# Row transform of an attention and Fourier-mixing kernel: fp32 products in place of a high and a low fp16 part

## The chip, the core and the metric

The kernel runs on one core of a Trainium2 chip. The core has TensorE (PE in the profile; PEld are its weight loads), VectorE (DVE), ScalarE (ACT), GpSimd (POOL) and SyncE (SP), which issues transfers. Each engine follows its own list of instructions in order. The metric is the device time of one launch in microseconds (us), a median over runs. SBUF is the memory beside the engines, PSUM the banks that TensorE writes products to.

## The reference

Two stages, for 4 batches, 8 heads, 768 rows and 64 values a head (8 x 64 = 512 columns):

```python
# attention in chunks of 32 rows, 16 rows of context before, 8 after, and 8 memory rows
scores = scale * np.matmul(q_c, k_full.transpose(0, 1, 3, 2))
a = np.exp(scores - np.max(scores, axis=-1, keepdims=True))
a = a / (np.sum(a, axis=-1, keepdims=True) + 1e-09)
out[:, :, c_start:c_end] = np.matmul(a, v_full)
# the heads side by side: x is (4, 768, 512)
mixed = np.real(np.fft.fft(np.fft.fft(x, axis=1), axis=2))
u = x + mixed
un = (u - mean(u)) / np.sqrt(var(u) + 1e-06)          # over the 512 columns
y = u + np.maximum(un @ w_ch1, 0.0) @ w_ch2           # 512 -> 2048 -> 512
```

The Fourier transform over the 768 rows is what the change touches. It is a sum over rows with tables of cosines and sines, so it can be done as matrix products.

## The kernel before, in words

The real part of the two-dimensional transform is symmetric, and the kernel folds the data first. For a batch, x (xs[b]) lies as 6 tiles of 128 rows by 512 columns. Columns c and c+256 are added and subtracted (zy): the sums carry the even output columns (par = 0), the differences the odd ones (par = 1). Rows r and r+384 are added and subtracted (pq): three row tiles each for even and odd row frequencies (sp = 0, 1). Columns are folded once more onto their mirror image (ff): a sum or a difference (ab = 0 for the cosine table, ab = 1 for the sine table), 128 columns each. What is left for a pair (par, ab) is 2 x 3 products (sp, and three row tiles st), each with a table of 128 rows by 193 columns (cosS, sinS). For par = 0 there is also one single column, 128, that folds onto itself and is done with six products of one column. Call six products (sp, st) a group.

Tables and data of these products are fp16. So that nothing is lost, ff (fp32) is split: ScalarE casts it to fp16 (hi, in e_hi and g_hi), VectorE subtracts (lo, in e_lo and g_lo), and TensorE takes each product twice, once with hi and once with lo, into the same PSUM bank (ps). In the profile these are lines 589 (batches 1 to 3), and 729, 735 and 748 (batch 0). ScalarE and VectorE split the result the same way into up (lines 601 and 606), and column products with tables cosD and sinD follow (pm, lines 759 and 780).

Batch 0 is done in another way (first_fourier, the functions whose names begin with g_), since its attention arrives half by half: g = 0 are row tiles 0 to 2, g = 1 tiles 3 to 5. There rows r and r+384 are not folded; each half is multiplied as it arrives, and for odd row frequencies of the second half a negated table (odd) is used. So a pair (par, ab) has 2 x 6 products, each with hi and with lo. The single columns (mid) are split on GpSimd. Their bank is first written by one product of zeros (line 729).

The other work on TensorE: the attention's turning of q and k (trq, trk, line 409), scores (sc, lines 465 and 488), values (xa and xo, line 517, in fp32), the first layer (ph, line 897), the last layer (pc, lines 915 and 964). In line 517 two products of 64 columns are written to the two halves of the partitions:

```python
nc.tensor.matmul(xa[64 * half:64 * half + 64, st, hh, 0:65],
                 e1[:, hh, t6, :], v1[:, hh, 6 * g + t6, 0:65],
                 start=True, stop=True)
```

For most pairs of row tiles (FAST) the last layer's 128x256 products (line 964) are saved by sums S that VectorE makes of the hidden values (line 952), and VectorE adds each bank to the rows (line 969).

The order of instructions is worked out when the program is built. A class Plan holds every step as a task: engine, a cost in us, the tasks it comes after, and the buffers it takes and gives back (take, give; their numbers are the slots of Plan, such as fold=2, un=6). Plan.order places tasks on the engines by rank and readiness, and Plan.shortest tries 24 variations of the ranks and keeps the one with the earliest end by those costs. The products of the last two layers are fillers that TensorE takes when nothing ranked higher is ready. Early on, before enough data is there, TensorE is given products of zeros (idle, line 1024). Buffers that matter here: fold (2 of 6 KB a partition; zy, pq, ff, later mix), hi and lo, un (normalised rows), unT (the same turned, two row tiles each), hT (hidden values).

Of the kernel before, what the change touches and what calls it, by code (L numbers as in the profile page):

```python
# [11 lines left out]
FP32 = mybir.dt.float32  # L12
BF16 = mybir.dt.bfloat16
# [193 lines left out]
def kernel(  # L207
# [70 lines left out]
    MIXED = 1  # L278
    cp_q = "p h j d -> p h (j d)"
# [5 lines left out]
                     xsb=3, fold=2, hl=1, up=4, dn=1, acc=2, mlp=2, un=6, unT=5, hT=1, S=1, room=2))  # L285
# [5 lines left out]
    mkf = fpool.tile([P, 2, D], FP32, tag="un", bufs=6, name="mkf")  # L291
    mkb = fpool.tile([P, 2 * D], BF16, tag="un", bufs=6, name="mkb")
# [11 lines left out]
    ident = fpool.tile([P, P], FP32, tag="un", bufs=6, name="ident")  # L304
# [231 lines left out]
    zy_of, pq_of, ff_of, hl_of, ps_of, up_of, pm_of, un_of, tp_of, dn_of, xr_of = ({} for _ in range(11))  # L536
    mu_of, unT_of, rs_of, rstd_of, g_of = ({} for _ in range(5))
    mid = cpool.tile([P, 2, NST, 1], FP16)
    mid32 = cpool.tile([P, NST, 1], FP32)
    warm = cpool.tile([P, 1], FP32)  # L540
# [18 lines left out]
    def e_ff(b, par, ab):  # L559
        pq = pq_of[b, par]  # L560
        if ab == 0:
            ff_of[b, par] = fpool.tile([P, 2, NST, P], FP32, tag="fold", bufs=2, name="ff")
        ff = ff_of[b, par]
        op = ALU.add if ab == par else ALU.subtract
        nc.vector.tensor_copy(ff[:, ab, :, 0], pq[:, :, P * ab])
        nc.vector.tensor_tensor(ff[:, ab, :, 1:P], pq[:, :, 1:P],  # L566
                                rev_ap(pq, HD - 1, P - 1, [[HD, NST]]), op)

    def e_hi(b, par, ab):
        if ab == 0:  # L570
            hl_of[b, par] = (fpool.tile([P, 2, NST, P], FP16, tag="hi", bufs=1, name="hi"),
                             fpool.tile([P, 2, NST, P], FP16, tag="lo", bufs=1, name="lo"))
        fl = "p b c -> p (b c)"
        nc.scalar.copy(hl_of[b, par][0][:, ab].rearrange(fl), ff_of[b, par][:, ab].rearrange(fl))  # L574

    def e_lo(b, par, ab):
        hi, lo = hl_of[b, par]
        fl = "p b c -> p (b c)"
        nc.vector.tensor_tensor(lo[:, ab].rearrange(fl), ff_of[b, par][:, ab].rearrange(fl),
                                hi[:, ab].rearrange(fl), ALU.subtract)  # L580

    def e_rows(b, par, ab):
        ps_of[b, par, ab] = ps = bank("acc", [P, 2, NK], FP32, "ps")

        def dft(out_, tab, c0, c1):
            for sp in range(2):
                for st in range(3):
                    for i, part in enumerate(hl_of[b, par]):
                        nc.tensor.matmul(out_[:, sp, :], part[:, ab, sp * 3 + st, c0:c1],  # L589
                                         tab[:, sp, st, :], start=(st == 0 and i == 0),  # L590
                                         stop=(st == 2 and i == 1))
# [107 lines left out]
    def g_hl(par, which):  # L699
        if (par, 0) not in g_of:  # L700
            if par == 0:
                g_of[0, 0] = fpool.tile([P, 2, NST, P], FP16, tag="hi", bufs=1, name="hi0")
                g_of[0, 1] = fpool.tile([P, 2, NST, P], FP16, tag="lo", bufs=1, name="lo0")
            else:
                both = fpool.tile([P, 2, 2, NST, P], FP16, tag="hT", bufs=1, name="hl1")
                g_of[1, 0], g_of[1, 1] = both[:, 0], both[:, 1]
        return g_of[par, which]

    def g_hi(par, ab, g):
        sl = slice(3 * g, 3 * g + 3)  # L710
        nc.scalar.copy(g_hl(par, 0)[:, ab, sl], ff_of[0, par][:, ab, sl])

    def g_lo(par, ab, g):
        sl = slice(3 * g, 3 * g + 3)
        nc.vector.tensor_tensor(g_hl(par, 1)[:, ab, sl], ff_of[0, par][:, ab, sl],
                                g_hl(par, 0)[:, ab, sl], ALU.subtract)

    def g_mid(g):
        sl = slice(3 * g, 3 * g + 3)
        xb = xs[0][:, sl]  # L720
        nc.gpsimd.tensor_tensor(mid32[:, sl], xb[:, :, P:P + 1], xb[:, :, HD + P:HD + P + 1],
                                ALU.add)
        nc.gpsimd.tensor_copy(mid[:, 0, sl], mid32[:, sl])
        nc.gpsimd.tensor_tensor(mid[:, 1, sl], mid32[:, sl], mid[:, 0, sl], ALU.subtract)

    def g_row(g):
        if g == 0:
            ps_of[0, 0, 1] = bank("acc", [P, 2, NK], FP32, "ps")
            nc.tensor.matmul(ps_of[0, 0, 1].rearrange("p s k -> p (s k)"), dz,
                             strided(dz, 0, [[0, NK], [1, 2]]), start=True, stop=False)  # L730
        for sp in range(2):
            one = odd[:, 0] if g == 1 and sp == 1 else cosS[:, sp]
            for st in range(3):
                for i in range(2):
                    nc.tensor.matmul(ps_of[0, 0, 1][0:1, sp, :], mid[:, i, 3 * g + st, :],
                                     one[:, st, :], start=False, stop=False)

    def g_rows(par, ab, g):
        if g == 0 and (par, ab) != (0, 1):
            ps_of[0, par, ab] = bank("acc" if par == 0 else "mlp", [P, 2, NK], FP32, "ps")  # L740
        ps = ps_of[0, par, ab]
        todo = []
        for sp in range(2):
            tab = odd[:, ab] if g == 1 and sp == 1 else (cosS, sinS)[ab][:, sp]
            todo += [(ps[:, sp, :], g_hl(par, i)[:, ab, 3 * g + st, :], tab[:, st, :])
                     for st in range(3) for i in range(2)]
        for m, (out_, data, tab) in enumerate(todo):
            nc.tensor.matmul(out_, data, tab, start=(g == 0 and m == 0 and (par, ab) != (0, 1)),  # L748
                             stop=(g == 1 and m == len(todo) - 1))
# [88 lines left out]
    def e_un(b, kt):  # L838
        un_of[b, kt] = un = fpool.tile([P, DM], FP16, tag="un", bufs=6, name="un")
# [23 lines left out]
    def unT(b, kt):  # L863
        i = kt if b == 0 else SLOT.index(kt)
        if (b, i // 2) not in unT_of:
            unT_of[b, i // 2] = fpool.tile([P, NDT, 2 * P], FP16, tag="unT", bufs=5, name="unT")
        return unT_of[b, i // 2][:, :, ts(i % 2, P)]
# [326 lines left out]
    def e_negatives():  # L1194
        for i, tab in enumerate((cosS, sinS)):
# [17 lines left out]
    t_neg = add("DVE", 0.6, e_negatives, [t_sines], rank=100)  # L1213
# [18 lines left out]
    def first_fourier():  # L1232
        t_rest, t_mid, t_row, pre = {}, {}, {}, {}
        for g in range(2):
# [18 lines left out]
            if g == 0:  # L1253
                for par in range(2):
                    for ab in range(2):
# [5 lines left out]
            t_row[g] = add("PE", 1.2, lambda g=g: g_row(g), [t_mid[g], t_neg, t_row.get(0), t_dz],  # L1261
                           take=("acc",) if g == 0 else ())
            for par in range(2):
                for ab in range(2):
# [8 lines left out]
                    if (par, ab, g) == (0, 0, 1):  # L1273
                        t_mark.append(ff)
                    hi = add("ACT", 0.5, lambda par=par, ab=ab, g=g: g_hi(par, ab, g),
                             [ff] + (pre[par, ab, 1][2:] if g == 1 else [pre[par, ab, 2]]),
                             take=(("hl",), ("hT",))[par] if (ab, g) == (0, 0) else ())
                    lo = add("DVE", 0.48, lambda par=par, ab=ab, g=g: g_lo(par, ab, g), [hi],
                             give=("fold",) if end else ())
                    if (par, ab, g) == (0, 0, 0):  # L1280
                        plan.filling = (t_sc[0, 0], add("PE", 0.0, lambda: let_go(fill_of[0]), [lo],
                                                        give=("mlp",)))
                    tag = ("acc", "mlp")[par]
                    mid_ = (par, ab) == (0, 1)
                    rw = add("PE", 1.0, lambda par=par, ab=ab, g=g: g_rows(par, ab, g),
                             [lo, t_neg] + ([t_row[g]] if mid_ else []),
                             take=(tag,) if g == 0 and not mid_ else (),
                             give=(("hl",), ("hT",))[par] if end else ())
# [9 lines left out]
    def fourier(b):  # L1298
# [7 lines left out]
        ff = hi = None  # L1306
        for par in range(2):
# [8 lines left out]
            for ab in range(2):  # L1316
                ff = add("DVE", 1.1, lambda par=par, ab=ab: e_ff(b, par, ab), [pq, prev],
                         take=("fold",) if ab == 0 else (), give=("fold",) if ab == 1 else ())
                prev = ff
                hi = add("ACT", 0.85, lambda par=par, ab=ab: e_hi(b, par, ab), [ff, hi],  # L1320
                         take=("hl",) if ab == 0 else ())
                lo = add("DVE", 0.96, lambda par=par, ab=ab: e_lo(b, par, ab), [hi],
                         give=("fold",) if ab == 1 else ())
                rw = add("PE", 2.2 if par == 0 and ab == 1 else 1.02,
                         lambda par=par, ab=ab: e_rows(b, par, ab), [lo, t_sines],
                         take=("acc",), give=("hl",) if ab == 1 else ())
# [265 lines left out]
```

## Time and profile before

| what | us |
|---|---|
| median of 3 runs (277.37 to 277.85) | 277.37 |
| the profiled execution, its own time | 277.39 |
| span in the profile, first to last instruction | 275.7 |
| TensorE busy | 258.7 |
| VectorE busy | 204.9 |
| ScalarE busy | 160.6 |
| GpSimd busy | 78.5 |

The granted TensorE clock is full speed throughout. The page divides the span into 40 slices of about 6.9 us and gives each engine's busy share in tenths. The chain of work is followed back from the last instruction: at each step to what released it, or to the instruction before it on its engine. In its list in order of time each line has the start, the length, the engine, the tile written and the line of the kernel, and how many instructions were merged. In lists by line, a name such as ps<-cosS,hi says what is written and read; 128*128 are active rows and columns of the array, 128x193 is the shape that streams through. A matmul's duration includes its run through the array; the next one starts before it ends.

### The profile page before, as it was taken

What the parts mean: (1) busy time and instruction counts of PE and PEld (TensorE: products, weight loads), DVE (VectorE), ACT (ScalarE), POOL (GpSimd) and SP (SyncE); (2) the same over time, 40 slices, a digit from 0 to 9 for tenths busy, and PEclk for the clock granted to TensorE, in tenths of its full rate; (3) what the DMA queues carried; (4) which work ended last, traced back from release to release, by engine and by line L of the source; (5) the groups of instructions that cost most, each with busy time, mean ns of one, the idle gap of its engine ahead of it and who ended that gap; (6) DMA issues with size and microseconds to landing.
All of it is one profiled execution on the core that took longest, in us unless ns stands there. A gap on an engine that the chain in (4) does not pass through costs nothing.

```text
span 275.7 us, 8160 instructions
## 1 busy us (share of the span) xinstructions
PE 258.7 (94%) x3365; PEld 209.8 (76%) x3365; DVE 204.9 (74%) x460; ACT 160.6 (58%) x300; POOL 78.5 (28%) x146
## 2 busy tenths in 40 slices
PE   0489999999999999999999989999999998999995
PEld 0367797888756788658669868888889887888884
DVE  7978999840337999998995997839997996354444
ACT  6888647888555688277646627555373483615150
POOL 8852652350111054045046246001100371000000
PEclk9999999999999999999999999999999999999999
DMA  6999999999997979958989964644960424313152
GB/s 104 203 176 176 193 211 205 198 195 200 174 190 176 204 170 175 212 79 160 241 144 199 183 118 117 123 117 146 132 182 1 95 62 83 111 40 76 64 90 76
DMA packets 116118, 39.98 MB, mean 145 GB/s; under 512 B 104561, under 2 KB 111473, under 8 KB 116081
## 3 DMA queue, kind: packets, MB, share of 16 engines
q1 hardware_dynamic: 93888, 23.54, 47.4%
q0 software_dynamic: 21472, 15.21, 34.8%
q10 hardware_dynamic: 720, 0.72, 0.8%
q8 instruction: 26, 0.43, 0.7%
q14 instruction: 12, 0.09, 0.1%
HBM read 37.36 MB, written 13.37 MB: 184 GB/s over the span
## 4 chain that ended last, share of the span: by engine, by line
PE 80%; DVE 11%; POOL 4%; ACT 2%; issue 1%; POOLq 0%; DVEq 0%
PE ph L897 26%; PE pc L964 14%; PE pc L915 10%; PE ps L589 6%; PE xa L517 5%; PE xo L517 4%; PE pm L759 3%; PE ps L748 3%; DVE S L952 2%; PE sc L465 2%; DVE st L832 2%; DVE xsb L969 2%; PE trk L409 2%; PE idle L1024 1%; PE trq L409 1%; DVE hT L952 1%
## 5 line engine op out<-in xcount | busy, mean ns | idle before, releaser
L897 PE MATMUL ph<-unT,w_sb 128*128 128x256 f16 x768 | 89.6, 273 | 0.0
L897 PEld LDWEIGHTS <-w_sb 128*128 128x128 f16 x768 | 73.7, 98 | 9.3 <-issue 0.3
L906 ACT ACTIVATE hT<-ph 128x512 f16<-128x512 f32 x96 | 56.3, 600 | 39.9 <-PE ph L897 21.1
L964 PEld LDWEIGHTS <-hT 128*128 128x128 f16 x320 | 30.8, 98 | 7.1 <-issue 2.0
L964 PE MATMUL pc<-w_sb,hT 128*128 128x256 f16 x256 | 32.1, 273 | 1.3 <-DVE xsb L969 0.9
L969 DVE TENSOR_TENSOR xsb<-pc,xsb 128x256 f32<-128x256 f32 x57 | 23.7, 420 | 12.6 <-PE pc L964 10.8
L915 PE MATMUL pc<-w_sb,hT 128*128 128x512 f16 x128 | 29.8, 380 | 0.0
L500 ACT ACTIVATE e<-sc,mbias 128x192 f32<-128x192 f32 (+1 forms) x48 | 19.2, 489 | 8.8 <-PE sc L488 8.8
L915 PEld LDWEIGHTS <-hT 128*128 128x128 f16 x128 | 11.8, 98 | 12.9 <-issue 0.4
L952 DVE TENSOR_TENSOR S<-hT 128x768 f16<-128x768 f16 (+1 forms) x16 | 8.5, 533 | 16.1 <-ACT hT L906 15.7
L475 ACT ACTIVATE e<-sc,mbias 128x384 f32<-128x384 f32 x32 | 17.0, 575 | 4.6 <-PE sc L465 4.3
L846 ACT ACTIVATE un<-xsb,rs 128x512 f16<-128x512 f32 x16 | 12.4, 810 | 9.8 <-POOL rs L861 9.8
L964 PE MATMUL pc<-w_t,S 128*128 128x256 f16 x128 | 16.0, 273 | 1.3 <-DVE xsb L969 1.1
L832 DVE BATCH_NORM_STATS2 st<-xsb 128x6 f32<-128x512 f32 x24 | 16.3, 680 | 0.3
L820 POOL TENSOR_TENSOR xsb<-mix,xr 128x512 f32<-128x512 f32 x6 | 8.7, 1459 | 26.6 <-ACT mix L814 26.6
L517 PEld LDWEIGHTS xa<-va,e 128*64 128x64 f32 x384 | 12.9, 142 | 3.8 <-issue 2.7
L601 ACT CAST up<-ps 128x386 f16<-128x386 f32 x16 | 9.7, 606 | 10.4 <-PE ps L589 9.4
L964 PEld LDWEIGHTS <-S 128*128 128x128 f16 x128 | 12.3, 98 | 3.7 <-issue 1.6
L517 PE MATMUL xa<-va,e 128*64 128x65 f32 x384 | 15.2, 230 | 0.0
L517 PE MATMUL xo<-va,e 128*64 128x65 f32 x384 | 14.1, 223 | 0.0
L574 ACT CAST hi<-ff 128x768 f16<-128x768 f32 x12 | 9.7, 829 | 6.3 <-DVE ff L566 6.1
L517 PEld LDWEIGHTS xo<-va,e 128*64 128x64 f32 x384 | 12.6, 138 | 0.5 <-ACT ff L683 0.3
(189 smaller groups left out, 471.9 us busy)
## 6 DMA issues: line engine op xcount, KB each, us to landing
va<-in_v_dram SPq DMA_DIRECT2D x32, 220.0 KB
w_sb<-in_moe_w_ch_dram POOLq DMA_DIRECT2D x8, 512.0 KB, 15.7
out_dram<-xsb SPq DMA_DIRECT2D x12, 256.0 KB
qs<-in_q_dram POOLq DMA_DIRECT2D x12, 192.0 KB, 6.4
ks<-in_k_dram POOLq DMA_DIRECT2D x12, 192.0 KB, 6.9
x_rows<-xsb POOLq DMA_DIRECT2D x3, 768.0 KB, 4.5
xr<-x_back POOLq DMA_DIRECT2D x3, 768.0 KB, 6.0
out_rows<-xsb SPq DMA_DIRECT2D x9, 256.0 KB
```

Of the source, the lines that this page charges most:

```text
L475: nc.scalar.activation(e1[:, :, :, ts(half, 32)], sc[:, :, 0:6, ts(half, 32)], AFT.Exp, bias=mbias[:, half:half + 1], scale=1.0 / math.sqr ...
L500: nc.scalar.activation(to, src, AFT.Exp, bias=mbias[:, half:half + 1], scale=1.0 / math.sqrt(D))
L517: nc.tensor.matmul(xa[64 * half:64 * half + 64, st, hh, 0:65], e1[:, hh, t6, :], v1[:, hh, 6 * g + t6, 0:65], start=True, stop=True)
L589: nc.tensor.matmul(out_[:, sp, :], part[:, ab, sp * 3 + st, c0:c1], tab[:, sp, st, :], start=(st == 0 and i == 0), stop=(st == 2 and i == 1))
L832: nc.vector.bn_stats(st6, xs[b][:, kt, :])
L846: nc.scalar.activation(un, xs[b][:, kt, :], AFT.Identity, bias=rs[:, 1:2], scale=rs[:, 0:1])
L897: nc.tensor.matmul(ph[:, k, :], w1_sb[:, dt, ts(HH * k + i, P)], unT_of[b, j][:, dt, :], start=(dt == 0), stop=(dt == NDT - 1))
L906: nc.scalar.activation(hT_of[b, j][:, :, i, :], ph, AFT.Relu, bias=0.0, scale=1.0 if (b, j) in FAST else -1.0)
L915: nc.tensor.matmul(pc_of[b, j, r], hT_of[b, j][:, k, i, ts(r, P)], w2_sb[:, HH * k + i, :], start=(i + k == 0), stop=(i + k == HH))
L952: nc.vector.tensor_tensor(out_[:, lo:hi], a[:, lo:hi], c[:, lo:hi], op)
L964: nc.tensor.matmul(pc_of[key], a[:, i, :], w[:, i, :], start=(i == 0 and new), stop=(i == HH - 1), skip_group_check=not new)
L969: nc.vector.tensor_tensor(u, pc, u, ALU.add)
```

## The change

The row products take ff itself, in fp32, with fp32 tables. The split into hi and lo goes, on ScalarE, VectorE and (for the single columns) GpSimd, and each product is issued once. cosS, sinS and odd become fp32; odd moves to the buffer of hT. In batches 1 to 3 ff is one tile for each (par, ab) in buffers of its own (tag ff, two of 3 KB), which the row products give back, where it lay in fold and lo gave that back.

In batch 0 the even columns (FOLDED = (0,)) are folded over rows r and r+384 ahead of the products, by two VectorE operations for each ab (g_fold), and then go through e_rows like the other batches. The odd columns stay unfolded, half by half. The single columns are folded by two GpSimd operations (g_midf) and multiplied in one group (g_row) after the second pair's products; the product of zeros goes.

To make room, un goes from 6 to 5 buffers and unT from 5 to 4. The costs that the plan has for a group stay as they were.

```diff
+    FOLDED = (0,)
-                     xsb=3, fold=2, hl=1, up=4, dn=1, acc=2, mlp=2, un=6, unT=5, hT=1, S=1, room=2))
+                     xsb=3, fold=2, hl=2, up=4, dn=1, acc=2, mlp=2, un=5, unT=4, hT=1, S=1, room=2))
...
-    cosS = wpool.tile([P, 2, 3, NK], FP16)
-    sinS = wpool.tile([P, 2, 3, NK], FP16)
-    odd = wpool.tile([P, 2, 3, NK], FP16)
+    cosS = wpool.tile([P, 2, 3, NK], FP32)
+    sinS = wpool.tile([P, 2, 3, NK], FP32)
+    odd = None
...
-        if ab == 0:
-            ff_of[b, par] = fpool.tile([P, 2, NST, P], FP32, tag="fold", bufs=2, name="ff")
+        ff_of[b, par, ab] = ff = fpool.tile([P, NST, P], FP32, tag="ff", bufs=2, name="ff")
...
-        nc.scalar.copy(hl_of[b, par][0][:, ab].rearrange(fl), ff_of[b, par][:, ab].rearrange(fl))
...
-        nc.vector.tensor_tensor(lo[:, ab].rearrange(fl), ff_of[b, par][:, ab].rearrange(fl),
-                                hi[:, ab].rearrange(fl), ALU.subtract)
...
     def e_rows(b, par, ab):
...
-                    for i, part in enumerate(hl_of[b, par]):
-                        nc.tensor.matmul(out_[:, sp, :], part[:, ab, sp * 3 + st, c0:c1],
-                                         tab[:, sp, st, :], start=(st == 0 and i == 0),
-                                         stop=(st == 2 and i == 1))
+                    nc.tensor.matmul(out_[:, sp, :], ff_of[b, par, ab][:, sp * 3 + st, c0:c1],
+                                     tab[:, sp, st, :], start=st == 0, stop=st == 2)
...
-        if par == 0 and ab == 1:
+        if b and par == 0 and ab == 1:
             dft(ps[0:1], cosS, 0, 1)
...
+    def g_midf():
+        for sp, op in ((0, ALU.add), (1, ALU.subtract)):
+            nc.gpsimd.tensor_tensor(midf[:, 3 * sp:3 * sp + 3], mid32[:, 0:3], mid32[:, 3:6], op)
+
+    def g_row():
+        ps = ps_of[0, 0, 1]
+        for sp in range(2):
+            for st in range(3):
+                nc.tensor.matmul(ps[0:1, sp, :], midf[:, 3 * sp + st, :], cosS[:, sp, st, :],
+                                 start=st == 0, stop=st == 2)
+
+    def g_fold(par, ab):
+        ff = ff_of[0, par][:, ab]
+        ff_of[0, par, ab] = full = fpool.tile([P, NST, P], FP32, tag="ff", bufs=2, name="full")
+        for sp, op in ((0, ALU.add), (1, ALU.subtract)):
+            nc.vector.tensor_tensor(full[:, 3 * sp:3 * sp + 3], ff[:, 0:3], ff[:, 3:6], op)
...
-            todo += [(ps[:, sp, :], g_hl(par, i)[:, ab, 3 * g + st, :], tab[:, st, :])
-                     for st in range(3) for i in range(2)]
+            todo += [(ps[:, sp, :], ff_of[0, par][:, ab, 3 * g + st, :], tab[:, st, :]) for st in range(3)]
...
+        odd = fpool.tile([P, 2, 3, NK], FP32, tag="hT", bufs=1, name="odd")
...
-    t_neg = add("DVE", 0.6, e_negatives, [t_sines], rank=100)
+    t_neg = add("DVE", 0.9, e_negatives, [t_sines], rank=100)
...
+                    if par in FOLDED:
+                        if g == 0:
+                            continue
+                        fd = add("DVE", 0.97, lambda par=par, ab=ab: g_fold(par, ab),
+                                 full + pre[par, ab, 0, "full"], take=("hl",),
+                                 give=("fold",) if ab else ())
+                        rw = add("PE", 1.0, lambda par=par, ab=ab: e_rows(0, par, ab), [fd, t_sines],
+                                 take=(tag,), give=("hl",))
+                    else:
+                        rw = add("PE", 1.0, lambda par=par, ab=ab, g=g: g_rows(par, ab, g),
+                                 full + [t_neg], take=(tag,) if g == 0 else (),
+                                 give=("fold",) if end else ())
```

More of the change, by code (lines that the diff above doesn't have):

```diff
@@ L533, in e_norm @@
             let_go(xa)
-    zy_of, pq_of, ff_of, hl_of, ps_of, up_of, pm_of, un_of, tp_of, dn_of, xr_of = ({} for _ in range(11))
+    zy_of, pq_of, ff_of, ps_of, up_of, pm_of, un_of, tp_of, dn_of, xr_of = ({} for _ in range(10))
     mu_of, unT_of, rs_of, rstd_of, g_of = ({} for _ in range(5))
-    mid = cpool.tile([P, 2, NST, 1], FP16)
     mid32 = cpool.tile([P, NST, 1], FP32)
+    midf = cpool.tile([P, NST, 1], FP32)
     warm = cpool.tile([P, 1], FP32)
@@ L697, in g_both @@
                                 ALU.add if ab == par else ALU.subtract)
[L699 to L716, printed above, removed]
     def g_mid(g):
@@ L722, in g_mid, with g_rows @@
                                 ALU.add)
-        nc.gpsimd.tensor_copy(mid[:, 0, sl], mid32[:, sl])
-        nc.gpsimd.tensor_tensor(mid[:, 1, sl], mid32[:, sl], mid[:, 0, sl], ALU.subtract)
-    def g_row(g):
-        if g == 0:
[L728 to L739, printed above, removed]
+    def g_midf():
[12 more added lines that the diff above has]
+            nc.vector.tensor_tensor(full[:, 3 * sp:3 * sp + 3], ff[:, 0:3], ff[:, 3:6], op)
+    def g_rows(par, ab, g):
+        if g == 0:
             ps_of[0, par, ab] = bank("acc" if par == 0 else "mlp", [P, 2, NK], FP32, "ps")
@@ L744, in g_rows @@
             tab = odd[:, ab] if g == 1 and sp == 1 else (cosS, sinS)[ab][:, sp]
-            todo += [(ps[:, sp, :], g_hl(par, i)[:, ab, 3 * g + st, :], tab[:, st, :])
-                     for st in range(3) for i in range(2)]
+            todo += [(ps[:, sp, :], ff_of[0, par][:, ab, 3 * g + st, :], tab[:, st, :]) for st in range(3)]
         for m, (out_, data, tab) in enumerate(todo):
-            nc.tensor.matmul(out_, data, tab, start=(g == 0 and m == 0 and (par, ab) != (0, 1)),
+            nc.tensor.matmul(out_, data, tab, start=(g == 0 and m == 0),
                              stop=(g == 1 and m == len(todo) - 1))
@@ L1274, in first_fourier @@
                         t_mark.append(ff)
[L1275 to L1279, printed above, removed]
+                    full = [ff] + (pre[par, ab, 1][2:] if g == 1 else [pre[par, ab, 2]])
                     if (par, ab, g) == (0, 0, 0):
-                        plan.filling = (t_sc[0, 0], add("PE", 0.0, lambda: let_go(fill_of[0]), [lo],
+                        plan.filling = (t_sc[0, 0], add("PE", 0.0, lambda: let_go(fill_of[0]), [ff],
                                                         give=("mlp",)))
                     tag = ("acc", "mlp")[par]
[L1284 to L1288, printed above, removed]
+                    pre[par, ab, g, "full"] = full
+                    if par in FOLDED:
[10 more added lines that the diff above has]
+                                 give=("fold",) if end else ())
+                    if (par, ab, g) == (0, 1, 1):
+                        mf = add("POOL", 0.5, g_midf, list(t_mid.values()), rank=20)
+                        rw = add("PE", 1.0, g_row, [rw, mf])
                     if g == 1:
@@ L1305, in fourier @@
         zy = {}
-        ff = hi = None
+        ff = None
         for par in range(2):
@@ L1317, in fourier @@
                 ff = add("DVE", 1.1, lambda par=par, ab=ab: e_ff(b, par, ab), [pq, prev],
-                         take=("fold",) if ab == 0 else (), give=("fold",) if ab == 1 else ())
+                         take=("hl",), give=("fold",) if ab == 1 else ())
                 prev = ff
[L1320 to L1323, printed above, removed]
                 rw = add("PE", 2.2 if par == 0 and ab == 1 else 1.02,
-                         lambda par=par, ab=ab: e_rows(b, par, ab), [lo, t_sines],
-                         take=("acc",), give=("hl",) if ab == 1 else ())
+                         lambda par=par, ab=ab: e_rows(b, par, ab), [ff, t_sines],
+                         take=("acc",), give=("hl",))
                 up = add("ACT", 0.6, lambda par=par, ab=ab: e_up(b, par, ab), [rw], take=("up",))
```

28 lines of the change are left out of this document (9 added, 19 removed).

## The prediction

> **What bounds the kernel now.** I read the page first, then the chain of work that ended last, then the waits, then the instructions of single lines. The page's busy line and slices, and the chain's share by engine:
>
> ```profile
> PE 258.7 (94%) x3365; PEld 209.8 (76%) x3365; DVE 204.9 (74%) x460; ACT 160.6 (58%) x300; POOL 78.5 (28%) x146
> PE   0489999999999999999999989999999998999995
> DVE  7978999840337999998995997839997996354444
> PE 80%; DVE 11%; POOL 4%; ACT 2%; issue 1%; POOLq 0%; DVEq 0%
> ```
>
> TensorE (PE) is busy from slice 3 to slice 38, and the chain runs through it for 80% of the span. So from about 31 us on, a microsecond more or less of TensorE work is a microsecond of the end, except where TensorE waits for VectorE (DVE). Where the row products stand in the chain (start, length, what), batch 0 first, then batch 2:
>
> ```profile
> 31.69 0.27 PE ps L729
> 31.96 1.10 PE ps L735 x12
> 33.06 4.26 PE ps L748 x48
> 37.33 1.10 PE ps L735 x12
> 38.43 4.14 PE ps L748 x48
> ...
> 133.50 1.01 PE ps L589 x12
> ...
> 137.78 2.22 PE ps L589 x24
> ...
> 177.07 0.85 PE xa L517 x24
> 177.92 0.70 PE xo L517 x24
> ```
>
> All row products are on the chain: 10.87 us for batch 0 (the five pieces), and for batches 1 to 3 5.34, 5.36 and 5.17 us of L589 pieces, 15.87 together. Sum 26.74 us. Twelve products of a 193-column fp16 table take 1.01 us, 0.084 each. The last two lines are the fp32 products that the kernel already has, those of the values; they price the new ones. Single lines, with least, median and greatest duration of one in ns, and two grouped rows with the mean:
>
> ```profile
> L488 PE MATMUL sc<-qT,kTb x192: 190/190/200, 86.9 to 179.9; 64*128 64x64 bf16 x192
> L517 PEld LDWEIGHTS xo<-va,e x384: 132/138/138, 18.2 to 184.9; 128*64 128x64 f32 x192
> L517 PE MATMUL xo<-va,e x384: 222/222/272, 18.3 to 185.0; 128*64 128x65 f32 x192
> L897 PE MATMUL ph<-unT,w_sb 128*128 128x256 f16 x768 | 89.6, 273 | 0.0
> L729 PE MATMUL ps<-dz 128*128 128x386 bf16 x1 | 0.3, 337 | 0.0
> ```
>
> What TensorE still waits for in the later stages (total, times, longest), and what the change takes off VectorE and ScalarE:
>
> ```profile
> PE pc L964 <- DVE xsb L969: 2.0, 5, 0.5
> PE pc L964 <- DVE hT L952: 0.4, 1, 0.4
> PE pc L964 <- DVE S L952: 0.2, 1, 0.2
> L579 DVE TENSOR_TENSOR lo<-ff,hi 128x768 f16<-128x768 f32 x12 | 11.3, 952 | 1.2 <-ACT hi L574 1.1
> L574 ACT CAST hi<-ff 128x768 f16<-128x768 f32 x12 | 9.7, 829 | 6.3 <-DVE ff L566 6.1
> ```
>
> **The price of an fp32 product.** The program issues 192 products xo, and the trace has 384 records: each fp32 product is two. Durations of 16-bit products rise by 0.42 ns a column (273 ns at 256 columns, 190 at 64). An fp32 record of 65 columns takes 222 ns, 31 more than 65 columns of 16 bits would: as if some 140 columns went by, two for each. The chain agrees if two run side by side: one after another at 140 columns, 24 records would take 24 x 59 = 1.41 us, and they took 0.70. The code has that: e_values writes each second product to the other 64 columns of the array. A row product uses all 128 columns, so nothing runs beside it. Its record is then 2 x 193 = 386 columns, at the 0.425 ns a column that 256 columns take in the chain (eight L897 products, 0.87 us): 0.164 us. One product is 0.328 us against 0.168 for the high and the low one that it replaces; a group of six is 1.97 us against 1.01.
>
> By the Trainium skill ("FP8 and Floating Point Precision", TensorE Precision Notes) true fp32 is four passes through the array; that page would give the same sum, and the two records at two columns a column agree.
>
> **The sum, part by part.**
>
> Row products of batches 1 to 3 (e_rows): five groups a batch (four, and the single column at the end), 15 x 1.97 = 29.5 us in place of 15.87.
>
> Row products of batch 0: even columns folded first, so two groups; odd columns not folded, four; the single columns, folded, one; the product of zeros (0.27) goes. 7 x 1.97 = 13.8 us in place of 10.87. The fold saves five groups and still doesn't pay for the price.
>
> Together 22 groups, 43.3 - 26.74 = +16.6 us, all on the chain.
>
> Entering fp32: xa, which follows other work, took 0.85 us, and xo behind it 0.70, so 0.15 for each block of fp32 products that follows 16-bit ones. The built order has 10 such blocks: +1.5 us. Bounds 0 and 3.0 (some blocks follow value products, some lie alone). Sum so far +18.1.
>
> VectorE: twelve lo subtractions of 0.952 go (11.4 us), eight of 0.547 in batch 0 (4.4); four folding operations come, like those subtractions 128x384 (2.2), and two negations in fp32 (the fp16 ones took 0.70 together; a fp32 tensor_scalar of 1158 took 0.765, so some 1.0). Net -13.3 us. ScalarE: 12 x 0.829 and 8 x 0.512 go, -14.0 us. GpSimd: four operations of 0.29 go, two come. These engines are off the chain but for 11%, so this is worth only what TensorE waits for VectorE: 2.6 us in seven waits by the rows above, plus a matmul's run-out of some 0.17 that each wait lays open (0.17 x 7), 3.8 us. Those waits come when the output of the column products (mix, xsb, st) and the sums S of the last layer crowd VectorE, not at the lo steps. Bounds 0 and -3.8; I take -2.0, half, since the added TensorE time lies just ahead of these places and lets VectorE catch up, while the crowd itself stays.
>
> Steps at nothing, with their cover. The negations (+0.3) lie on VectorE at 13 to 14 us, ahead of a kTb copy whose scores ScalarE, busy from 14 to 20 us, takes up late; without that cover 0.3. In batch 0 the folds wait for both halves of the sequence, but the odd columns' first two groups (3.9 us on TensorE from about 32.7) lie ahead of them in the built order, and by my count of 0.47 us an operation the first fold is done near 35.6; uncovered, 1 us. The folded single columns are two GpSimd operations behind the second mid; behind them wait the w1 loads, whose data is wanted at 51 us, now later. In batches 1 to 3 the third ff now needs a buffer that TensorE gives back with the first group; behind it on VectorE stand bank reads of the last layer, but the read of that group's own result stands ahead of it in the order already, so it adds no wait. The order is planned with 1.0 us for a group that I price at 1.97; queues are followed in order, so this delays but does not starve TensorE.
>
> 277.39 (the profiled execution; its span 275.7, 1.7 outside it; the median of the runs is 277.37) + 18.1 - 2.0 = 293.5 us.
>
> **The rivals.**
>
> Other side: an fp32 product costs twice a 16-bit one in all, no more than the pair it replaces. Place: the row products. The trace allows it only if the value products run one after another: 0.70/24 = 29 ns is also 65 columns at the fp16 rate. Against it stand the 222 ns. Then 22 x 1.01 + 1.5 - 26.74 - 2.0 = -5.0: 272.4 us. It decides below (26.74 + 2.0 - 1.5) / 264 = 0.103 us a record. The Trainium skill ("Perfetto Trace Analysis", Engine Utilization) puts FP32_LOW_HIGH at half the array's output rate; read for a whole product that is this rival, read for each record it is my forecast. Chance 4%.
>
> Between: the same, but the weight load sets the pace. 64 fp32 columns loaded in 138 ns, against 82 to 84 for one column: 56 ns for 64, so 112 for 128. A group is 1.34 us; 22 x 1.34 + 1.5 - 26.74 - 2.0 = +2.2: 279.6 us. Chance 4%.
>
> Worse: a 128-column fp32 load does not run beside a product, 0.164 + 0.112 a record, 3.31 a group: 72.8 + 1.5 - 26.74 - 2.0 = +45.6: 323 us. Against it, the value products keep their pace with a load for each. Chance 3%.
>
> New wait: the buffers of normalised rows shrink (un 6 to 5, unT 5 to 4), and a pair of tiles comes late to the first layer. Two transposing loads at 1.23 us to issue and one un of 0.81 make 3.3 us a time; if it strikes in batches 2 and 3 with no stall recovered, 302 us; once, 298.5 with half of the recovery lost. SP is seldom the releaser of TensorE in the waits. Chance 9%.
>
> **Numbers.** Forecast as summed 80%, its own range 289 (every stall gone, no cost on entry) to 297.5. Range 287.5 to 298.5, which takes in the milder new wait. 0.2% is about what a measurement here can tell from no change. Faster 4%, within 0.2% 1%, slower 95%.
>
> **What will show it.** Row products: records doubled against the program's, near 327 to 337 ns each (386 columns, as the row of L729), a group of 12 records near 1.97 us in the chain; 110 ns apart would be the middle rival, 84 the other side. TensorE's 94% stays or rises, VectorE falls to about 192 us and ScalarE to 147. Waits of the pc products on VectorE should shrink, not vanish. TensorE waiting for unT would be the new wait. I am wrong if records of row products follow at much less than 160 ns, or if the slices show TensorE no longer full.

## The result and the profile after

The changed kernel takes 296.22 us (median of 4 runs, 296.21 to 296.60), the kernel before beside it 277.61 (4 runs, 277.37 to 277.85). The ratio is 1.0674, with a 95% interval of 1.0655 to 1.0692: slower by 18.6 us. The profiled execution took 296.22, its span 294.5, so the span is 18.8 longer.

The page of the changed kernel: busy time by engine, the slices of TensorE (PE) and VectorE (DVE), the chain's share by engine, and the group in which ScalarE copies the results of the row products (busy, mean ns | idle before it, and what ended it):

```profile
PE 277.3 (94%) x3328; PEld 225.4 (77%) x3328; DVE 193.5 (66%) x444; ACT 148.2 (50%) x280; POOL 77.3 (26%) x144
PE   0599899999999999999999999999999999999995
DVE  7979935950339865599736995645975898172534
PE 84%; DVE 9%; POOL 4%; issue 1%; ACT 1%; DVEq 0%; POOLq 0%
L585 ACT CAST up<-ps 128x386 f16<-128x386 f32 x16 | 9.6, 601 | 31.5 <-PE ps L574 25.6
```

TensorE took the whole of it: 277.3 - 258.7 = 18.6 us more busy time, the same 94% of a longer span. VectorE and ScalarE lost 11.4 and 12.4 us. What ScalarE lost came back as waiting: its up copies alone now stand 25.6 us for the row products of L574, where they stood 9.4 us for those of L589 before.

The row products in the chain of work that ended last, in order of time (start, length, what), with what stands ahead of those of batch 0:

```profile
31.17 0.49 PE trk L410 x16
...
31.68 1.04 ACT kTb L453
...
32.90 4.18 PE ps L715 x24
37.08 0.46 PE trq L410 x16
37.54 2.17 PE ps L574 x12
...
39.99 2.17 PE ps L574 x12
42.15 2.06 PE ps L697 x12
44.21 4.13 PE ps L715 x24
...
102.70 2.24 PE ps L574 x12
106.68 6.30 PE ps L574 x36
...
115.23 2.16 PE ps L574 x12
...
141.71 6.00 PE ps L574 x36
150.40 3.94 PE ps L574 x24
```

Twelve records, six products, are 1.97 us in the last line (3.94 for 24) and 2.06 to 2.24 in the pieces of twelve: there a record at the start or the end takes longer. Batch 0 has 14.7 us, batch 1 10.7, batches 2 and 3 9.9 each (batch 3 repeats the 6.00 and 3.94): 45.3 in place of 26.7.

Single lines of the changed kernel, weight loads and products (least, median, greatest ns); the second pair is the single columns of batch 0:

```profile
L574 PEld LDWEIGHTS ps<-cosS,ff x108: 79/188/193, 102.7 to 225.4; 128*128 128x128 f32 x72, 128*1 128x1 f32 x36
L574 PE MATMUL ps<-cosS,ff x108: 324/326/431, 102.7 to 225.6; 128*128 128x193 f32 x72, 128*1 128x193 f32 x36
L697 PEld LDWEIGHTS ps<-cosS,midf x12: 80/83/86, 42.1 to 43.7; 128*1 128x1 f32 x12
L697 PE MATMUL ps<-cosS,midf x12: 324/326/328, 42.1 to 43.9; 128*1 128x193 f32 x12
```

A record of 193 columns takes 326 ns whether 128 columns of weights were loaded for it (188 ns) or one (83 ns). The waits of TensorE from 31 us on (total, times, longest):

```profile
PE ps L715 <- ACT ff L667: 1.3, 1, 1.3
PE pc L931 <- DVE xsb L936: 1.1, 3, 0.5
PE ph L864 <- ACT hT L873: 0.9, 2, 0.7
PE pc L931 <- DVE hT L919: 0.4, 1, 0.4
PE pm L726 <- DVE xsb L791: 0.2, 1, 0.2
```

The waits of the pc products for VectorE shrank from 2.6 to 1.5 us, and 2.4 us of other waits appeared: 3.9 in 8, where there were 2.6 in 7. To put the whole span together I gave each TensorE record the time from its start to the next record's start and added this up by tile:

| TensorE time by tile | after less before, us |
|---|---|
| row products (ps), 26.9 to 45.3 | +18.4 |
| turning of k (trk), with the wait behind it | +1.6 |
| last layer (pc), with its waits | -1.1 |
| products of zeros (idle) | -1.0 |
| scores and values | +1.2 |
| everything else | -0.2 |
| span, 275.7 to 294.5 (the parts are rounded) | +18.8 |

### The profile page after: what moved, and what is told of

The parts are those of the page before. It is cut to its first block, busy times and chain, and to the rows that moved or that the text cites. A ratio compares the mean times of both kernels' runs of the same rounds, so it can differ in the third digit from the quotient of the medians.

```text
span 294.5 us, 8048 instructions
## 1 busy us (share of the span) xinstructions
PE 277.3 (94%) x3328; PEld 225.4 (77%) x3328; DVE 193.5 (66%) x444; ACT 148.2 (50%) x280; POOL 77.3 (26%) x144
## 3 DMA queue, kind: packets, MB, share of 16 engines
q0 software_dynamic: 21472, 15.21, 31.6%
## 4 chain that ended last, share of the span: by engine, by line
PE 84%; DVE 9%; POOL 4%; issue 1%; ACT 1%; DVEq 0%; POOLq 0%
PE ph L864 26%; PE pc L931 14%; PE ps L574 12%; PE pc L882 10%; PE xa L518 4%; PE xo L518 4%; PE ps L715 3%; PE pm L726 2%; PE sc L466 2%; DVE st L799 2%; PE idle L991 2%; PE trk L410 1%; PE trq L410 1%; PE pm L747 1%; PE sc L489 1%
## 5 line engine op out<-in xcount | busy, mean ns | idle before, releaser
L936 DVE TENSOR_TENSOR xsb<-pc,xsb 128x256 f32<-128x256 f32 x57 | 23.8, 422 | 13.6 <-PE pc L931 11.7
L585 ACT CAST up<-ps 128x386 f16<-128x386 f32 x16 | 9.6, 601 | 31.5 <-PE ps L574 25.6
L590 DVE TENSOR_TENSOR up<-ps,up 128x386 f16<-128x386 f32 x16 | 9.6, 599 | 22.0 <-ACT up L585 22.0
L919 DVE TENSOR_TENSOR S<-hT 128x768 f16<-128x768 f16 (+1 forms) x16 | 7.8, 490 | 24.3 <-ACT hT L873 23.8
L882 PEld LDWEIGHTS <-hT 128*128 128x128 f16 x128 | 11.6, 97 | 13.3 <-issue 0.8
L574 PE MATMUL ps<-cosS,ff 128*128 128x193 f32 (+1 forms) x108 | 19.3, 328 | 0.1
L574 PEld LDWEIGHTS ps<-cosS,ff 128*128 128x128 f32 (+1 forms) x108 | 14.5, 154 | 4.0 <-issue 1.0
L428 ACT COPY qT<-trq 128x768 bf16<-128x768 bf16 x12 | 9.5, 796 | 11.1 <-PE trq L410 11.1
## 6 DMA issues: line engine op xcount, KB each, us to landing
w_sb<-in_moe_w_ch_dram POOLq DMA_DIRECT2D x8, 512.0 KB, 15.1
```

The lines of the kernel that those rows point to most:

```text
L574: nc.tensor.matmul(out_[:, sp, :], ff_of[b, par, ab][:, sp * 3 + st, c0:c1], tab[:, sp, st, :], start=st == 0, stop=st == 2)
L585: nc.scalar.copy(up[:, 0].rearrange("p k s -> p s k"), ps_of[b, par, ab])
L882: nc.tensor.matmul(pc_of[b, j, r], hT_of[b, j][:, k, i, ts(r, P)], w2_sb[:, HH * k + i, :], start=(i + k == 0), stop=(i + k == HH))
L936: nc.vector.tensor_tensor(u, pc, u, ALU.add)
```

## The experiments

In all of them the kernel before ran beside the others on the same chip: 277.75 us for the third of the row tiles, the smaller buffers, the odd columns first and the true costs, 277.69 for the other four. "After" is the changed kernel, 296.22, which was measured beside 277.61.

**The price of a product: a third of the row tiles.** Leaves out two of the three row tiles in batches 1 to 3, 60 products; the transform of these batches is not the whole one.

```diff
-                for st in range(3):
+                for st in range(1 if b else 3):
-                                     tab[:, sp, st, :], start=st == 0, stop=st == 2)
+                                     tab[:, sp, st, :], start=st == 0, stop=st == (0 if b else 2))
```

> The changed kernel with two of the three row tiles left out of each row product sum in batches 1 to 3 (so the transform of these batches is not the whole one): 15 groups of six products become two products each, 60 fp32 products fewer. Theory (0.328 us a product, TensorE full, one to one): 60 x 0.328 = 19.7 us less than the changed kernel, 276.5 us, give or take 1.5 for waits on VectorE that come into the open. Rival (part of the added time is waits or order, not the products): the gain is under 15 us, 281 us or more, with TensorE waiting for VectorE's ff or up.

Measured: 281.08 us, ratio 1.0117 (1.0095 to 1.0139), 15.1 less than after. By its total this is the number of the rival, and 3 us above what theory allowed. By its trace it is not the rival: the row products fell from 45.3 to 26.1 us, 19.2 for the 60 products (120 records) left out, 0.160 a record. The other 4 us were spent elsewhere. The chain from 150 us on:

```profile
151.73 1.67 POOL qs L378 x2
...
155.55 1.30 POOL xsb L787
...
156.87 0.16 ACT mix L761
...
157.09 0.51 ACT hT L873
...
157.64 4.46 PE ph L864 x24
```

and TensorE in the same stretch (window, us, busy and count, granted clock, DMA share, GB/s):

```profile
154.00:157.00 3.00, 0.42 (x16) 1.00 1.87 176
157.00:158.00 1.00, 0.36 (x3) 0.95 2.12 155
158.00:159.00 1.00, 1.00 (x7) 0.50 2.21 166
...
160.00:161.00 1.00, 1.00 (x6) 0.50 2.26 231
...
162.00:163.00 1.00, 1.00 (x11) 1.00 0.43 31
```

With its row work gone, TensorE gets to the first layer early and finds nothing: GpSimd is issuing loads of q and k, its xsb stands behind them, ScalarE's mix behind that, and hT behind that. TensorE is busy for 0.42 of 3 us, and then the clock is granted at half from 157.9 to 161.3. So the products cost on the chain what they take; what stands next in line took 4 of the 19 us back.

**Does the weight load set the pace? Each product in two of 97 and 96 columns.** The streamed columns stay, the loads double (batch 0's odd columns and single columns are as after).

```diff
-                for st in range(3):
-                    nc.tensor.matmul(out_[:, sp, :], ff_of[b, par, ab][:, sp * 3 + st, c0:c1],
-                                     tab[:, sp, st, :], start=st == 0, stop=st == 2)
+                for k0, k1 in ((0, 97), (97, NK)):
+                    for st in range(3):
+                        nc.tensor.matmul(out_[:, sp, k0:k1], ff_of[b, par, ab][:, sp * 3 + st, c0:c1],
+                                         tab[:, sp, st, k0:k1], start=st == 0, stop=st == 2)
```

> The changed kernel with each product of e_rows (batches 1 to 3, and batch 0's even columns) in two, of 97 and 96 columns, so the same columns stream by in all and each 128-column weight load is done twice. A 128-column fp32 load takes 188 ns in the changed kernel, a one-column load 79, so the columns take some 0.109 us. Theory (a record takes the longer of its columns' 2 x 97 x 0.417 = 0.081 us and its load's 0.109): 14 groups with 128-column weights go from 1.97 to 24 x 0.110 = 2.64 us, 9.4 us more, 305.6 us, while the single columns' records, with short loads, follow at 0.083 us. Rival (loads are always hidden): 24 x 0.084 = 2.0 us a group, 296 to 297 us. Other rival (loads and columns add up): 24 x 0.19 a group, 330 us or more.

Measured: 306.08 us, ratio 1.1022 (1.0998 to 1.1045), 9.9 more than after, where theory gave 305.6. Its single lines for the sine table, loads and products:

```profile
L575 PEld LDWEIGHTS ps<-sinS,ff x144: 186/192/192, 108.8 to 237.5; 128*128 128x128 f32 x144
L575 PE MATMUL ps<-sinS,ff x144: 274/275/351, 108.8 to 237.6; 128*128 128x97 f32 x72, 128*128 128x96 f32 x72
```

Such records follow each other at 0.110 to 0.113 us. Streaming alone would be 97 / 193 of 0.164, 0.082. The single columns of batches 1 to 3, split in the same way but with one-column loads, do follow at 0.081 to 0.087. So what sets the 0.110 is the load: a 128-column load takes 192 ns and a one-column load 83, and the difference is 109. So the load does have the price of the second rival (0.112), and it sets the pace of short products; at 193 columns it lies wholly under the 0.164 of streaming.

**Do the smaller buffers cost?** The kernel before with un 6 to 5 and unT 5 to 4, in the plan and in the pools.

```diff
-                     xsb=3, fold=2, hl=1, up=4, dn=1, acc=2, mlp=2, un=6, unT=5, hT=1, S=1, room=2))
+                     xsb=3, fold=2, hl=1, up=4, dn=1, acc=2, mlp=2, un=5, unT=4, hT=1, S=1, room=2))
...
-        un_of[b, kt] = un = fpool.tile([P, DM], FP16, tag="un", bufs=6, name="un")
+        un_of[b, kt] = un = fpool.tile([P, DM], FP16, tag="un", bufs=5, name="un")
...
-            unT_of[b, i // 2] = fpool.tile([P, NDT, 2 * P], FP16, tag="unT", bufs=5, name="unT")
+            unT_of[b, i // 2] = fpool.tile([P, NDT, 2 * P], FP16, tag="unT", bufs=4, name="unT")
```

> The kernel before with un at 5 buffers and unT at 4, nothing else changed. Theory (the products' price explains the change, the buffers nothing): within 0.5 us of the kernel before, 277.0 to 278.0 us, TensorE waits as before. Rival (fewer buffers bring a pair late to the first layer, and some of the 18.6 us are theirs): 279 us or more, and TensorE's first-layer products wait for unT.

Measured: 277.78 us, ratio 1.0007 (0.9993 to 1.0022). The buffers cost nothing that can be measured.

**The new wait at 31.6 us: odd columns first in the first half.** After, with the pairs of the first half in the other order; the work is the same.

```diff
-            for par in range(2):
+            for par in ((1, 0), (0, 1))[g]:
...
-                         take=("dn",) if (par, g) == (0, 0) else ())
+                         take=("dn",) if (par, g) == (1, 0) else ())
...
-                    if (par, ab, g) == (0, 0, 0):
+                    if (par, ab, g) == (1, 0, 0):
                         plan.filling = (t_sc[0, 0], add("PE", 0.0, lambda: let_go(fill_of[0]), [ff],
```

> The changed kernel, with the odd columns' ff of batch 0's first half made ahead of the even ones on VectorE; TensorE's order is the same. In the changed kernel TensorE ends its trk at 31.6 us and starts the first row products at 32.9, when VectorE has made the odd ff, third in its order. Theory (this 1.2 us wait is on the chain, since the single columns that stood there before are now at the end): first row products at about 31.7 us, 1.2 us faster than the changed kernel, 295.0 us. Rival (what follows waits for VectorE anyway, the folds or the column sums): no faster, 296.0 to 296.4 us, with the wait moved to the fold or to pm.

Measured: 295.24 us, ratio 1.0630 (1.0608 to 1.0651), 1.0 less than after. The chain of this kernel where the row products of batch 0 start:

```profile
30.54 0.56 DVE ff L654
...
31.24 0.57 DVE xsb L529
...
31.94 4.18 PE ps L715 x24
```

The same 4.18 us piece starts at 31.94 in place of 32.90, the end comes 1.0 earlier, and so does what follows it. That wait was on the chain, one to one.

**The fold undone: batch 0's even columns unfolded, the rest as after.**

```diff
-    FOLDED = (0,)
+    FOLDED = ()
```

> The changed kernel without the fold of batch 0's even columns (the single columns stay folded): fp32 alone, without the second part of the change. TensorE gets two groups of six more, 2 x 1.97 = 3.9 us, VectorE four operations of 0.55 less, and the even columns' first half can start without the 1.3 us wait at 31.6 us. Theory (TensorE's list decides): 296.2 + 3.9 - 1.3 = 298.8 us, 298 to 300. Rival (the folding operations and their wait cost as much as they save): 296 us or less.

Measured: 299.96 us, ratio 1.0799 (1.0773 to 1.0826), 3.7 more than after. The chain of this kernel at the start of the row products:

```profile
31.52 2.05 PE ps L715 x12
33.56 0.47 PE trk L410 x16
34.04 10.04 PE ps L715 x60
```

It has two groups more: its row products take 48.9 us, 3.5 more than after. Its products start at 31.52, so the 1.3 us wait is gone, but its later waits are longer (a pc product alone waits 1.1 us for VectorE's hT), and the gain is lost again. That is the even columns' fold alone; the single columns stay folded.

**The fold without fp32: batch 0's even columns and single columns folded, then split into hi and lo.** The kernel before, with the fold in place ahead of the split.

```diff
+    def g_fold(ab):
+        ff = ff_of[0, 0][:, ab]
+        nc.vector.tensor_tensor(ff[:, 0:3], ff[:, 0:3], ff[:, 3:6], ALU.add)
+        nc.vector.scalar_tensor_tensor(ff[:, 3:6], ff[:, 3:6], -2.0, ff[:, 0:3], ALU.mult, ALU.add)
...
+                        fd = add("DVE", 1.1, lambda ab=ab: g_fold(ab), full + pre[par, ab, 0, "full"])
+                        hi = add("ACT", 0.85, lambda ab=ab: g_hi_full(ab), [fd],
...
+                        lo = add("DVE", 0.96, lambda ab=ab: g_lo_full(ab), [hi],
...
+                        rw = add("PE", 1.0, lambda ab=ab: g_rows_full(ab), [lo, t_sines],
...
+                            mf = add("POOL", 1.2, g_midf, list(t_mid.values()), rank=20)
+                            rw = add("PE", 1.0, g_row, [rw, mf])
```

> The kernel before with the fold alone: batch 0's even columns and single columns folded ahead of the products, in place and in fp32, then split into hi and lo as before. TensorE's list loses five groups of 1.01 us less two, and the product of zeros, some 3.9 us in all (10.87 to 7.1); VectorE gets four folding operations (2.1 us) in the stretch from 31 to 43 us, where it is busy 94% and each lo still waits for ScalarE. Theory (without fp32 VectorE sets the end of batch 0's rows, so the fold gives nothing): 276.5 to 279 us, with TensorE waiting for lo. Rival (the fold is worth its products here too, and only fp32 is the loss): 274.5 us or less.

Measured: 283.24 us, ratio 1.0206 (1.0172 to 1.0240). Slower than before, though TensorE has fewer products: both expectations were too low. The chain of this kernel:

```profile
33.83 0.94 DVE hl L715 x2
...
35.73 0.57 DVE ff L733
...
38.54 0.87 DVE lo L740
```

and TensorE in the same stretch (columns as above):

```profile
32.00:34.00 2.00, 0.73 (x17) 1.00 1.22 194
34.00:35.00 1.00, 0.65 (x8) 1.00 1.24 244
35.00:36.00 1.00, 1.00 (x11) 0.65 1.39 196
36.00:37.00 1.00, 1.00 (x8) 0.50 1.09 150
...
39.00:40.00 1.00, 1.00 (x20) 1.00 1.09 213
```

VectorE, which must fold (L733, L734) and then subtract lo (L715, L740), carries the chain from 30 to 40.8 us. TensorE is busy for 1.38 of 3 us, 1.3 us of the rest being a wait for a load of k, and from 35.3 to 38.7 the clock is granted at half. The row products took 25.4 us, only 1.5 less than before; trq, with the wait behind it, took 2.1 more and tp 1.1. Counted in their order, the products of the first layer start 2.75 us later than those of the kernel before at 154 to 157 us.

The other half of the loss comes later, in the last layer:

```profile
162.00:165.00 3.00, 1.05 (x9) 1.00 0.68 134
165.00:166.00 1.00, 1.00 (x7) 0.51 0.00 0
166.00:168.00 2.00, 2.00 (x12) 0.50 0.29 66
```

TensorE is thin once more, with a wait of 1.5 us for the sums S, the clock is granted at half from 165.0 to 168.4, and from there the products of the first layer start 5.4 us later than before. Whether this second stretch belongs to the fold or to the order that the plan chose was not tested.

**The single columns alone: folded, split, and multiplied in one group at the end.** The kernel before with nothing else changed; the product of zeros goes.

```diff
+    def g_midf():
+        for sp, op, f in ((0, ALU.add, sv), (1, ALU.subtract, svS)):
...
+                    if (par, ab, g) == (0, 1, 1):
+                        mf = add("POOL", 1.2, g_midf, list(t_mid.values()), rank=20)
+                        rw = add("PE", 1.0, g_row, [rw, mf])
```

> The kernel before with only batch 0's single columns folded (GpSimd, two operations more) and multiplied in one group at the end; the product of zeros goes, hi and lo stay. TensorE's list gets 1.03 + 0.27 us shorter, but the single columns no longer cover the 1.1 us in which the first lo is made. Theory (cover lost and list shortened cancel): 277.0 to 278.0 us, no change. Rival (the cover is found in other work): 276.4 us or less, faster than both kernels.

Measured: 278.84 us, ratio 1.0041 (1.0029 to 1.0054): 1.1 us slower than before, where theory allowed 277.0 to 278.0. The row products fell by 1.5 us, but the fill products of zeros grew by 0.9 and the first layer with its waits by 1.4. The saved TensorE work was more than lost in these two places. That the moved products had been the cover there is the likely reading, but what makes the first layer wait longer was not taken apart.

**The plan with the true costs.** After, with a group planned at 1.97 and 3.94 us in place of 1.0 and 2.2.

```diff
-                        rw = add("PE", 1.0, lambda par=par, ab=ab: e_rows(0, par, ab), [fd, t_sines],
+                        rw = add("PE", 1.97, lambda par=par, ab=ab: e_rows(0, par, ab), [fd, t_sines],
...
-                rw = add("PE", 2.2 if par == 0 and ab == 1 else 1.02,
+                rw = add("PE", 3.94 if par == 0 and ab == 1 else 1.97,
```

> The changed kernel with the plan's cost of a group of row products set to the measured 1.97 us (3.94 with the single column) in place of 1.0 (2.2); all else as in the changed kernel, so only the order differs. Theory (TensorE is full and its list is the same length, an order can only win the waits, some 4 us in all): 293.5 to 296.5 us. Rival (the changed kernel is slow because its order was planned with half the true cost): 290 us or less.

Measured: 297.08 us, ratio 1.0694 (1.0671 to 1.0718), 0.9 more than after and 0.6 above what theory allowed. The rival, that the order was what cost, falls. The waits of TensorE in this kernel:

```profile
PE pc L931 <- DVE xsb L936: 1.1, 3, 0.5
PE trq L410 <- ACT kTb L453: 1.1, 1, 1.1
PE trq L410 <- DMA qs<-in_q_dram: 0.8, 1, 0.8
...
PE ps L715 <- DVE ff L654: 0.4, 1, 0.4
```

The wait ahead of the first row products is down from 1.3 to 0.4 us, and two waits of trq have come, 1.9 us together. The order that this plan chose moves a microsecond from one place to another; none that was run moves the 18.

## Why the prediction was right, and where a term was off

296.2 lies in the range, 287.5 to 298.5, and in the forecast's own, 289 to 297.5; it is 2.7 us above the 293.5. Two of the bounds do not follow from their own terms: every stall gone and no cost on entry give 277.39 + 16.6 - 3.8 = 290.2, not 289, and the new wait once with half of the recovery lost gives 293.5 + 3.3 + 1.0 = 297.8, not 298.5. Point by point:

**What bounds the kernel.** Right. TensorE is busy 94% as before and carries 84% of the chain. The third of the row tiles shows it from the other side: the row products gave up 19.2 us and the end 15.1, with the rest lost to what stood next in line.

**The price of a product.** Right. Two records of 193 columns, 0.162 to 0.168 us each where I had 0.164; 326 ns long where I had 327 to 337; a group 1.97 us. By the Trainium skill ("FP8 and Floating Point Precision", TensorE Precision Notes) true fp32 is four passes; the trace agrees, with two records that each take two columns' time for a column. The half rate that the Trainium skill's "Perfetto Trace Analysis" (Engine Utilization) gives for FP32_LOW_HIGH fits each record here (0.164 us against 0.084), not the product (0.328).

**Products and entry.** +16.6 and +1.5, 18.1 together, against 18.4 measured, which is partly luck. The row products stand 2.0 us above 22 groups of 1.97, and two things make that. There are ten blocks, as I counted, but a first record takes longer (0.24 to 0.27 us to the next one's start, where others take 0.164) only eight times, two of them inside a block and none in batches 2 and 3: 0.8 us in place of 1.5. The other 1.2 us had no term in my sum: thirteen groups end with a record of 0.25 to 0.26 us. The kernel before has such ends too, thirteen records of 0.17 to 0.18 where others take 0.084, so its 26.7 held them and my 43.3 did not. What makes the last record of a group longer stays open.

**What VectorE and ScalarE lose.** 11.4 and 12.4 us of busy time, where I had 13.3 and 14.0. Added up instruction by instruction the loss is 13.6 and 14.7; busy time counts a stretch in which two records overlap once. Right was that it does not lie on the chain: ScalarE now stands idle ahead of row products instead.

**The term of -2.0 for the waits was the one that failed.** All TensorE time that is not row products came out at +0.4, not -2.0, with my bounds at 0 and -3.8. The part that I meant did happen, at 1.1 us: the waits of the pc products shrank from 2.6 to 1.5. What I left out is what came in its place. Among the steps put at nothing, I wrote of the odd columns' first two groups "from about 32.7", and in the lines of before that I showed the product of zeros and the first single columns fill 31.69 to 33.06. They were moved to the end of batch 0's products. So nothing covers ScalarE's 1.04 us kTb copy and the ff step behind it, and TensorE waits 1.3 us. I had the new start time and charged nothing for it. With the other order of columns this wait shrinks and the end comes 1.0 us earlier. Another 1.1 us of new waits (ph for hT, pm for xsb) and 1.2 us more in scores and values (0.6 each) were not isolated, but other runs narrow them. The kernel before on fewer buffers also has 0.9 us more in the values and 1.1 less in products of zeros, at an unchanged total, so that shift is not of the fp32 row products. With the plan of true costs the scores are back at the time of the kernel before, with the same fp32 products, so their 0.6 goes with the order. The wait of ph for hT is there, at 1.4 us, in the kernel with the single columns alone, so it does not need fp32; what makes it stays open.

**The folds at nothing.** Right for fp32: undoing the even columns' fold costs 3.7 us, near the two groups that come back (3.94). But it is no property of the fold. With the split into hi and lo kept, folding the even and the single columns costs 5.5 us (283.2 against 277.7); the single columns alone cost 1.1, and about half of the 5.5 comes at the later slow stretch, whose tie to the fold is not shown. That the fold pays here because the hi and lo steps went and VectorE had the time is the likely reading.

**The plan's too low costs at nothing.** Right: with true costs the kernel is 0.9 us slower, not faster.

**The rivals.** Half the rate in all (272.4) falls with the 0.164 us of a record. The weight load as the pace (279.6) falls with the single columns, whose one-column load leaves the pace as it is, and with the split products, where the load does set the pace, at 0.110 instead. The load that is not hidden (323) falls with the same. The new wait for rows or their turned copies falls with the kernel before on fewer buffers, 1.0007, and with the waits of the changed kernel, in which TensorE never stands for unT. None of the versions tried is faster than the kernel before.

## What to carry to other kernels

By these figures an fp32 product can pay in place of a high and a low fp16 product only where the split, and not TensorE, is the bound: here it is two records at half rate, 0.328 us against 0.168 for the pair, and beside a full TensorE the removal of 24 us of VectorE and ScalarE work came with only 1.1 us less in the last layer. When work is moved from the front of a stage to its end, look at what ran beside it: that is uncovered even where the moved work itself is saved. And ask of a fold that saves products whether the engine that folds has the time: in the kernel with hi and lo it carried the chain, and the saved products bought nothing.

## What the runs showed of the hardware that I had not expected

The fp32 load of 128 columns adds about 109 ns to that of one column (192 against 83) and sets a floor of 0.110 us a record: at 97 columns the load sets the pace (0.110 to 0.113 us, against 0.081 to 0.087 with a one-column load), at 193 the columns do. At 0.85 ns a column (0.164 / 193) the two meet near 130 columns, an estimate from these two rows.

The clock fell to half in runs where TensorE was not idle but merely thin. With a third of the row tiles TensorE had worked 0.27 of the last 3.41 us before the drop, with the fold and hi and lo 1.76 and, later, 1.47; each time the clock was granted at 0.50 for the next 3.41 us. Apart from these three places no stretch of 3.41 us between 20 us and the last 5 us had less than 2.04 us of work in any of the ten kernels (the least is that of the single columns alone, from 160.8 us), and there the clock stayed full. By the Trainium skill ("TensorE: Matmul & The Clock Gate", Part 1) the clock halves after an idle window of about 3.4 us and comes back after a busy one of that length; the length of the slow stretch agrees, 3.41 us three times, but all three windows here had work in them. So a thin stretch of that length can cost up to 1.7 us more behind it, half of the 3.41.
